# Short-K products as row pairs, and transposes moved to DMA, in a recurrent attention and GLU kernel

## Chip, cores, metric

One core of a Trainium2 chip; the rounds ran on several chips, each with the kernel before beside it. The metric is the device time of the kernel in microseconds (us), as the median of its runs; on one core no slow state appeared in any of the runs below. Engines are named as in the profile: PE is TensorE's products, PEld its weight loads, DVE is VectorE, ACT is ScalarE, POOL is GpSimd, SP issues the DMAs.

## The reference, cut to what matters

Two attention layers with a recurrent memory and two gated layers (GLU) run in the order attention, GLU, attention, GLU over 2048 tokens of width 448. The attention walks through 64 segments of 32 tokens; the memory (8 rows) that a segment's attention puts out is an input of the next segment.

```python
for s in range(n_seg):                       # 64 segments, strictly one after the other
    h = concatenate([mem, x[s]])             # 8 + 32 = 40 rows of 448
    q, k, v = h @ Wq, h @ Wk, h @ Wv         # 16 heads of 256
    p = softmax(mask(q @ k.T * scale))
    o = (p @ v) @ Wo
    mem = o[:8]                              # the recurrence
    outs.append(o[8:])
...
x = x + A(layernorm(x)); x = x + B(layernorm(x))     # twice; B is the GLU
```

## The kernel before

Setup folds the weights: M = Wq Wk^T for each head (448 x 7168 in all), N = Wv Wo. A step then computes T = M h (56 blocks of 128 outputs), scores h T, softmax, U = P h, the new output N U. The two layers run interleaved, layer two 4 segments behind layer one: 68 steps, 60 of which hold both layers (80 columns a product) and 8 only one (40 columns).

The contraction over 448 is cut into four pieces of K: 128, 128, 128 and 64. The fourth piece runs as a product of 128 rows too, of which 64 are zeros:

```python
def t_unit(self, t, c, u0, m):               # m blocks of 128 outputs into one PSUM bank
    ...
        return [MM(b[:, j * n:j * n + n], S.M[:, kt, 16 * c + u0 + j, :],
                   S.hT[:, pp, s, kt, l0:l1, :].rearrange("p l x -> p (l x)"), start=(kt == 0), stop=(kt == 3))
                for j in range(m) for kt in range(4)]
```

LayerNorm results and segment probabilities are transposed on TensorE and copied out of PSUM:

```python
def ln_transpose(self, i, wr):
    T = S.tile("R", 1)
    S.mm(lambda: [MM(T.b().bitcast(BF)[:, c * 128:c * 128 + 128], S.xn[:, i, c * 128:c * 128 + 128], S.ident[:, :], is_transpose=True)
                  for c in range(4)], ...)

def seg_pt(self, t):
    G = S.tile("R", 1)
    S.mm(lambda: [MM(G.b().bitcast(BF)[:, a * 128:a * 128 + 128], S.Ps[:, a, :], S.ident[:, :], is_transpose=True) for a in range(4)], ...)
    S.cp(lambda: S.PTs[:, :], lambda: G.b().bitcast(BF)[:, 0:512], 512, G.res(), [("PTs",)])
```

The hand-off of the recurrence takes the new memory as a sum of two bf16 parts (hi and lo) through small selecting products into hT, which is T's moving operand. Three copies do it, in both kernels:

```python
S.cp(lambda: S.hT[:, pp, s, 0:3, l0:l1, SEG:KEYS], lambda: v()[:, 0:3], 48, ..., eng=("dve",))
S.cp(lambda: S.hT[0:64, pp, s, 3, l0:l1, SEG:KEYS], lambda: v()[64:128, 3], 16, ..., eng=("act",))
S.cp(lambda: S.hT[64:128, pp, s, 3, l0:l1, SEG:KEYS], lambda: v()[64:128, 3], 16, ..., eng=("act",))
```

No instruction order is written down. When the kernel is built, a list scheduler with assumed durations picks, for each engine, the ready operation of the highest priority; a table of constants (`BIAS`) shifts the priority of each kind of work. That computed order, with the semaphores that it needs, is what runs. I call it the plan; it has a length of its own, which is an assumption and not a measurement.

Of the kernel before, what the change touches and what calls it, by code (L numbers as in the profile page):

```python
# [17 lines left out]
SEG = 32  # L18
KEYS = SEG + MEM
NSEG = 64  # L20
F = 1792
# [22 lines left out]
class _Sched:  # L44
# [107 lines left out]
BIAS = {  # L152
    "b_down": -5000.0, "b_layer": 2000.0, "ln_a": 41619.0, "p_t_mem": 500.0, "s_mem": 74990.0, "s_seg": 72560.0,
    "seg_pt": -859.0, "u_mem": -38520.0, "u_seg": 2000.0, "un": -37811.0,
}
# [19 lines left out]
class _Order:  # L175
# [69 lines left out]
    def run(self):  # L245
# [13 lines left out]
        while len(order) < total:  # L259
            best = None  # L260
            for e in self.ENGS:
# [27 lines left out]
                lim = max(f, t0) + (60.0 if e == "pe" else 40.0)  # L289
                t, o = max((x for x in lst if x[0] <= lim), key=lambda x: (x[1].prio, -x[0]))  # L290
                if best is None or (t, -o.prio) < (best[0], -best[2].prio):
# [87 lines left out]
class _Kernel:  # L379
# [16 lines left out]
    def alloc(self):  # L396
        self.M = self.sb("Mw", [128, 4, NO, 128])
        self.N = self.sb("Nw", [128, NO, D])
# [11 lines left out]
        self.TTm = self.sb("TTm", [128, 4, 2, 128])  # L410
        self.hT = self.sb("hT", [128, 2, 2, 4, 2, KEYS])
        self.hK = self.sb("hK", [128, 2, 2, D])
# [3 lines left out]
        self.ys = self.sb("ys", [128, 2, D])  # L416
        self.xBT = self.sb("xBT", [128, 4, 128])
        self.hB = self.sb("hB", [128, NFC, 128])
        self.gT = self.sb("gT", [128, 2, 512])
        self.Es = self.sb("Es", [128, 8, KEYS], F32)  # L420
# [87 lines left out]
    def setup(self):  # L508
# [47 lines left out]
        S.dve(lambda E: E.tensor_scalar(S.ident[:, :], cf[:, 0:128], 0.0, None, op0=ALU.is_equal), 128, [("Es",)], [("ident",)])  # L556
        S.pool(lambda E: E.memset(S.M[64:128, 3, 0:28, :], 0.0), 1800, (), [("Mz", 0)])
        S.dve(lambda E: E.memset(S.M[64:128, 3, 28:56, :], 0.0), 1800, (), [("Mz", 1)])
        for j in range(4):
# [36 lines left out]
        for i in range(H // 2):  # L596
# [13 lines left out]
            for odd in range(2):  # L610
                u, r = i + 8 * odd, slice(64 * odd, 64 * odd + 64)
                S.cp(lambda u=u: S.M[0:64, 3, u:48:16, :], lambda T=T, r=r: T.b()[r, 0:384].rearrange("p (c x) -> p c x", c=3), 384,
                     T.res(half=(odd,)), [("M", 3, u)])
                S.cp(lambda i=i, odd=odd: S.M[0:64, 3, 48 + i, 64 * odd:64 * odd + 64], lambda T=T, r=r: T.b()[r, 384:448], 64,
                     T.res(half=(odd,)), [("M", 3, 48 + i, odd)])
        S.Mkeys = [("M", kt, u) for kt in range(4) for u in range(16)] + [("M", kt, 48 + i, o) for kt in range(4) for i in range(8) for o in range(2)]
        S.Mkeys += [("Mz", 0), ("Mz", 1)]
        S.Nkeys = [("N", o) for o in range(NO)]
# [88 lines left out]
    def qdma(self, name, fn, wr, rd=()):  # L707
        self.q.add("dma", ("sp",), {"sp": 60.0}, fn, rd, wr, name=name)

# [3 lines left out]
    def start_mem(self, l):  # L713

        S = self
        t = LAG * l
        pp, s = (t // 2) % 2, t % 2
        S.cp(lambda: S.hT[:, pp, s, :, l, SEG:KEYS], lambda: S.mTc[:, :, :], 32, [("mTc",)], S.mkeys(pp, s, l, l + 1),
             eng=("pool",))
        r = slice(64 * l + 32, 64 * l + 40)  # L720
        S.cp(lambda: S.hK[r, pp, s, :], lambda: S.mNc[0:MEM, 0:D], D, [("mNc", 0)], [("hKm", pp, s, l)], eng=("pool",))
# [14 lines left out]

    def ln_transpose(self, i, wr):
        S = self
        T = S.tile("R", 1)
        S.mm(lambda: [MM(T.b().bitcast(BF)[:, c * 128:c * 128 + 128], S.xn[:, i, c * 128:c * 128 + 128], S.ident[:, :], is_transpose=True)  # L740
                      for c in range(4)], 4 * S.pitch(128), [("xn", i, 0), ("xn", i, 1), ("ident",)], T.res() + wr)
        return T

    def ln_a(self, p):
        S = self
        pp = p % 2
        S.ln(S.XA[:, p % 4, :], [("XA", p % 4, 0), ("XA", p % 4, 1)], 0, "lnA", 0)
        T = S.ln_transpose(0, [("hTx", pp, s) for s in range(2)])
        for s in range(2):
            S.cp(lambda s=s: S.hT[:, pp, s, :, :, 0:SEG],  # L750
                 lambda s=s: T.b().bitcast(BF)[:, 0:512].rearrange("p (c l s q) -> p c l s q", c=4, l=2, s=2)[:, :, :, s, :],
                 256, T.res(), [("hTx", pp, s)])
        for s in range(2):
            for l in range(2):
                a = 64 * l + 32 * s
                S.cp(lambda a=a, l=l, s=s: S.hK[64 * l:64 * l + 32, pp, s, :], lambda a=a: S.xn[a:a + 32, 0, 0:D], D,
                     [("xn", 0, 0)], [("hKx", pp, s, l)], eng=("pool",))

    def ln_b(self, p):
        S = self  # L760
        S.ln(S.XB[:, p % 2, :], [("XB", p % 2, i) for i in range(3)], 16, "lnB", 1)
        T = S.ln_transpose(1, [("xBT",)])
        S.cp(lambda: S.xBT[:, :, :].rearrange("p a b -> p (a b)"), lambda: T.b().bitcast(BF)[:, 0:512], 512, T.res(), [("xBT",)])


    def t_unit(self, t, c, u0, m):

        S = self
        pp, s = (t // 2) % 2, t % 2
        l0, l1 = S.layers(t)  # L770
        nl = l1 - l0
        n = nl * KEYS
        R = S.tile("R", 1)

        def mms():
            b = R.b()
            return [MM(b[:, j * n:j * n + n], S.M[:, kt, 16 * c + u0 + j, :],
                       S.hT[:, pp, s, kt, l0:l1, :].rearrange("p l x -> p (l x)"), start=(kt == 0), stop=(kt == 3))
                    for j in range(m) for kt in range(4)]

        rd = [("hTx", pp, s)] + S.mkeys(pp, s, l0, l1)
        if t == 0:
            rd = rd + S.Mkeys
        dst = [(nm, c, u0, half) for nm in ("TTm", "TTs") for half in ((0, 1) if c == 3 else (0,))]
        S.mm(mms, 4 * m * S.pitch(n), rd, R.res() + dst)
        src = lambda: R.b()[:, 0:m * n].rearrange("p (o l x) -> p o l x", o=m, l=nl)
        for half in ((0, 1) if c == 3 else (0,)):
# [9 lines left out]

    UNITS = [(3, 0, 4), (3, 4, 4)] + [(c, u, m) for c in range(3) for u, m in ((0, 6), (6, 5), (11, 5))]
    TKEYS = [(c, u, half) for c, u, m in UNITS for half in ((0, 1) if c == 3 else (0,))]

    def s_mem(self, t):
# [4 lines left out]
        C = S.tile("R", 1)  # L806
        S.mm(lambda: [MM(C.b()[:, l * KEYS:l * KEYS + KEYS], S.TTm[:, c, l, :], S.hT[:, pp, s, c, l, :], start=(c == 3), stop=(c == 2))
                      for l in range(l0, l1) for c in (3, 0, 1, 2)], 100.0 * nl,
             [("TTm",) + k for k in S.TKEYS] + [("hTx", pp, s)] + S.mkeys(pp, s, l0, l1), C.res())
        st = S.stat  # L810
# [12 lines left out]
    def s_seg(self, t):  # L823
# [5 lines left out]
        def mms():  # L829
            b = G.b()  # L830
            out = [MM(b[:, 0:8 * KEYS], S.ident[:, :], S.maskr[:, :], start=True, stop=False)]
            for l in range(l0, l1):
                for qd in range(4):
                    for c in (3, 0, 1, 2):
                        out.append(MM(b[:, (qd * 2 + l) * KEYS:(qd * 2 + l) * KEYS + KEYS],
                                      S.TTs[:, c, l, qd * 4:qd * 4 + 4, :].rearrange("p u q -> p (u q)"), S.hT[:, pp, s, c, l, :],
                                      start=False, stop=(l == l1 - 1 and qd == 3 and c == 2)))
            return out
# [22 lines left out]
    def seg_pt(self, t):  # L861
        S = self
        G = S.tile("R", 1)
        S.mm(lambda: [MM(G.b().bitcast(BF)[:, a * 128:a * 128 + 128], S.Ps[:, a, :], S.ident[:, :], is_transpose=True) for a in range(4)],
             4 * S.pitch(128), [("Ps",), ("ident",)], G.res() + [("gseq",), ("PTs",)])
        S.cp(lambda: S.PTs[:, :], lambda: G.b().bitcast(BF)[:, 0:512], 512, G.res(), [("PTs",)])

# [47 lines left out]
    def m_t(self, t):  # L915
# [12 lines left out]
        v = lambda: C.b()[:, 0:64].rearrange("p (c l q) -> p c l q", c=4, l=2)[:, :, l0:l1, :]  # L928
        S.cp(lambda: S.hT[:, pp, s, 0:3, l0:l1, SEG:KEYS], lambda: v()[:, 0:3], 48, C.res(), mk[:-2], eng=("dve",))
        S.cp(lambda: S.hT[0:64, pp, s, 3, l0:l1, SEG:KEYS], lambda: v()[64:128, 3], 16, C.res(half=(1,)), mk[-2:-1], eng=("act",))  # L930
        S.cp(lambda: S.hT[64:128, pp, s, 3, l0:l1, SEG:KEYS], lambda: v()[64:128, 3], 16, C.res(half=(1,)), mk[-1:], eng=("act",))

# [154 lines left out]
    def step(self, t):  # L1087
# [3 lines left out]
        if t > 0:  # L1091
            S.do("m_nat", t)
        for k in S.UNITS:
            S.do("t_unit", t, *k)
        if not last:
# [54 lines left out]
```

## Time and profile before

The median was 1664.21 us in the three runs given at first, and 1664.74 us (1664.17 to 1666.01) in four runs beside the changed kernel.

| | before |
|---|---|
| span of the profiled run | 1662.0 us |
| PE busy | 97% |
| DVE busy | 69% |
| ACT busy | 43% |
| hole of PE in 200 us of the middle | 1.5 us |

The prediction below shows the head, the stretches, the groups and the timeline. What it doesn't show is the list of waits of PE (each line: who waited, for whom, us in total, how often, longest). Most of the long list is setup; of the steps it has

```profile
PE b L127 <- DVE xn L733: 7.0, 31, 1.0
...
PE b L127 <- DVE lo L913: 1.8, 2, 1.5
...
PE b L127 <- DVE Ps L859: 1.7, 2, 1.5
...
PE b L127 <- ACT hT L696: 1.0, 2, 0.7
```

xn and Ps are what the transposes on TensorE wait for. The hand-off of the memory, lo and hT on ACT, is waited for only twice each in the whole run.

### The profile page before, as it was taken

The numbers are of one execution on the slowest core, as the hardware profiler recorded it, in microseconds if no ns is written. First come the engines' busy times: TensorE is split into PE (matmuls) and PEld (weight loads), VectorE is DVE, ScalarE is ACT, GpSimd is POOL, SyncE is SP. The second block draws the span as 40 slices with busy tenths as digits, with TensorE's granted clock in tenths as the row PEclk, the third lists the DMA queues.
The fourth block names the chain that finished last, engine by engine and source line by source line (L and its number), as shares of the span: only waits on it lengthen the run. The fifth ranks groups of instructions, "written<-read, shape, count | busy, mean of one in ns | idle before, by whom it ended". The sixth has DMA issues, their size and how long they took to land. (4 is left out here: it accounts for less than half of the span.)

```text
span 1662.0 us, 68199 instructions
## 1 busy us (share of the span) xinstructions
PE 1614.9 (97%) x30742; PEld 1192.9 (72%) x30742; DVE 1141.2 (69%) x3172; ACT 717.2 (43%) x2051; POOL 93.3 (6%) x156
## 2 busy tenths in 40 slices
PE   5999999999999999999999999999999999999998
PEld 2567777777776777777777777777677777766775
DVE  8757767666767767676776766676676767676665
ACT  4623443445343444544343444434334453433442
POOL 4000000000000000000000000000000000000000
PEclk8999999999999999999999999999999999999999
DMA  9710000000000000000000000000000000000000
GB/s 234 207 40 5 4 3 6 6 5 5 5 5 6 5 4 6 6 4 6 6 5 4 5 5 5 4 6 6 5 6 5 5 6 4 5 3 4 4 4 6
DMA packets 55762, 27.54 MB, mean 17 GB/s; under 512 B 44584, under 2 KB 54576, under 8 KB 55472
## 3 DMA queue, kind: packets, MB, share of 16 engines
q1 hardware_dynamic: 55120, 22.94, 5.7%
q8 instruction: 242, 3.96, 1.0%
q14 instruction: 48, 0.39, 0.1%
q10 hardware_dynamic: 352, 0.24, 0.1%
HBM read 10.33 MB, written 1.84 MB: 7 GB/s over the span
## 5 line engine op out<-in xcount | busy, mean ns | idle before, releaser
L127 PEld LDWEIGHTS b<-hT,Mw 128*128 128x128 bf16 x15232 | 535.2, 100 | 16.9 <-issue 8.6
L127 PE MATMUL b<-hT,Mw 128*128 128x80 bf16 (+1 forms) x15232 | 544.0, 199 | 3.2 <-issue 1.8
L127 PE MATMUL b<-Nw,big 128*64 128x448 bf16 (+1 forms) x1936 | 307.8, 355 | 0.6 <-DVE big L697 0.5
L697 DVE CAST TTs<-b 128x320 bf16<-128x320 f32 (+5 forms) x542 | 244.8, 454 | 13.2 <-PE b L127 12.5
L127 PE MATMUL b<-xBT,big 128*128 128x128 bf16 (+1 forms) x3920 | 217.1, 214 | 0.4 <-DVE lo L913 0.4
L127 PEld LDWEIGHTS b<-xBT,big 128*128 128x128 bf16 x3920 | 203.2, 98 | 7.2 <-ACT UTm L696 4.8
L127 PEld LDWEIGHTS b<-Nw,big 128*64 128x64 bf16 (+1 forms) x1936 | 128.8, 104 | 105.7 <-issue 14.0
L127 PE MATMUL b<-Nw,UTm 128*32 128x448 bf16 x3752 | 193.1, 357 | 2.1 <-DVE UTm L697 1.0
L696 ACT ACTIVATE TTm<-b 64x64 bf16<-64x64 f32 (+5 forms) x338 | 76.7, 227 | 266.7 <-PE b L127 262.7
L1053 DVE TENSOR_TENSOR hB<-gT,b 128x256 bf16<-128x256 bf16 x227 | 91.1, 412 | 119.4 <-ACT gT L1052 108.2
L127 PEld LDWEIGHTS b<-Nw,UTm 128*32 128x32 bf16 x3752 | 100.8, 97 | 88.7 <-issue 15.7
L697 POOL COPY hK<-xn 32x448 bf16<-32x448 bf16 x136 | 75.9, 558 | 1466.9 <-DVE xn L733 1460.4
L696 ACT ACTIVATE TTs<-b 64x256 bf16<-64x256 f32 (+4 forms) x342 | 141.4, 413 | 30.3 <-PE b L127 24.2
L697 DVE CAST TTm<-b 128x80 bf16<-128x80 f32 (+5 forms) x546 | 126.0, 233 | 38.9 <-PE b L127 10.2
L696 ACT ACTIVATE big<-b 128x512 bf16<-128x512 f32 (+1 forms) x242 | 124.5, 555 | 30.7 <-PE b L127 29.9
L697 DVE CAST UTm<-b 128x448 bf16<-128x448 f32 (+2 forms) x124 | 80.2, 647 | 81.0 <-PE b L127 80.1
L1052 ACT ACTIVATE gT<-b 128x256 bf16<-128x256 f32 x227 | 85.6, 380 | 90.7 <-PE b L127 73.0
L697 DVE CAST big<-b 128x512 bf16<-128x512 f32 (+1 forms) x146 | 85.4, 596 | 25.0 <-PE b L127 22.6
L127 PE MATMUL b<-big,hB 128*128 128x448 bf16 (+1 forms) x490 | 98.8, 354 | 0.0
L912 ACT ACTIVATE hi<-b 128x448 bf16<-128x448 f32 x67 | 36.5, 544 | 121.4 <-PE b L127 119.8
L127 PE MATMUL b<-PTs,hK 40*128 40x512 bf16 (+1 forms) x640 | 83.6, 346 | 4.8 <-ACT PTs L696 1.5
L696 ACT ACTIVATE UTm<-b 128x448 bf16<-128x448 f32 (+2 forms) x127 | 64.6, 523 | 24.4 <-PE b L127 23.3
(105 smaller groups left out, 1503.3 us busy)
## 6 DMA issues: line engine op xcount, KB each, us to landing
big<-in_A_Wo_dram SPq DMA_DIRECT2D x3, 896.0 KB, 5.8
out_dram<-ys SPq DMA_DIRECT2D x32, 56.0 KB, 1.9
big<-in_B_W_down_dram SPq DMA_DIRECT2D x1, 1568.0 KB, 7.1
XA<-in_A_x_dram SPq DMA_DIRECT2D x28, 56.0 KB, 2.2
big<-in_B_W_up_dram SPq DMA_DIRECT2D x1, 1344.0 KB, 5.9
big<-in_B_W_gate_dram SPq DMA_DIRECT2D x1, 1344.0 KB, 8.8
Nw<-in_A_Wo_dram SPq DMA_DIRECT2D x1, 896.0 KB, 6.4
XA<-in_A_x_dram ACTq DMA_DIRECT2D x4, 56.0 KB, 4.3
```

The lines of the kernel that those rows point to most:

```text
L127: ins = E.matmul(out, lhsT=lhsT, rhs=rhs, **kw)
L696: return E.activation(out(), src(), ACT.Copy)
L697: return E.tensor_copy(out(), src())
L912: S.act(lambda E: E.activation(S.hi[:, :], C.b()[:, 0:D], ACT.Copy), D, C.res(), [("hi",)])
L1052: S.act(lambda E, k=k, R=R, n=n: E.activation(S.gT[:, k % 2, 0:n], R[0].b()[:, 0:n], ACT.Relu), n, R[0].res(), [("gT", k % 2)])
L1053: S.dve(lambda E, k=k, R=R, n=n, fcs=fcs: E.tensor_tensor(S.hB[:, fcs[0]:fcs[-1] + 1, 0:w], S.gT[:, k % 2, 0:n].rearrange("p (a b) -> p a ...
```

## The change

The intent: pack two 64-row pieces into one pass of the array (rows 0 to 63 and rows 64 to 127 as two tiles), which saves 25 of 224 product slots per step; and take the transposes off TensorE. To keep the number of row-mode switches low, T is cut into a block of six banks, a block of four and one single bank, each paired block starting with its row pairs. The scheduler gets a "stay" bonus for work in the mode that TensorE is in, and a new set of constants.

```diff
 BIAS = {
-    "b_down": -5000.0, "b_layer": 2000.0, "ln_a": 41619.0, ...
+    "b_down": -43294.0, "b_layer": -38803.0, "ln_b": 34745.0, ..., "stay": 42356.0, "t_block": 47423.0, ...
 }
-                t, o = max((x for x in lst if x[0] <= lim), key=lambda x: (x[1].prio, -x[0]))
+                stay = BIAS.get("stay", 0.0) if e == "pe" else 0.0
+                t, o = max((x for x in lst if x[0] <= lim), key=lambda x: (x[1].prio + stay * (x[1].mode == mode), -x[0]))
 ...
-        self.M = self.sb("Mw", [128, 4, NO, 128])
+        self.M = self.sb("Mw", [128, 3, NO, 128])
+        self.M3 = self.sb("M3", [128, 31, 128])
 ...
-        self.hT = self.sb("hT", [128, 2, 2, 4, 2, KEYS])
+        self.hT = self.sb("hT", [128, 2, 4, 2, 2, KEYS])
 ...
-        T = S.ln_transpose(1, [("xBT",)])
-        S.cp(lambda: S.xBT[:, :, :].rearrange("p a b -> p (a b)"), lambda: T.b().bitcast(BF)[:, 0:512], 512, T.res(), [("xBT",)])
+        S.tdma("xBT", lambda: S.xBT[:, :, :], lambda: S.xn[:, 1, :], [("xn", 1, 0), ("xn", 1, 1)], [("xBT",)])
 ...   (the same for xAT, whose DVE copies into hT stay, and for PTs)
+    def tdma(self, name, out, src, rd, wr):
+        self.q.add("dma", ("sp",), {"sp": 1250.0}, lambda E: E.dma_start_transpose(out=out(), in_=src()), rd, wr, name=name, lat=1150.0)
 ...
+    def t_block(self, t, units):
+        ...
+        R = [S.tile("R", 1) for _ in units]
+        pair = len(units) > 1
+        def first():
+            for a, b in zip(range(0, len(units), 2), range(1, len(units), 2)):
+                for j in range(units[a][2]):
+                    for x in (a, b):
+                        c, u0, m = units[x]
+                        side, slot = S.PLACE[16 * c + u0 + j]
+                        h = slice(64 * side, 64 * side + 64)
+                        out.append(MM(R[x].b()[:, j * n:j * n + n], S.M3[h, slot, :], mov(3, h), start=(j == 0), stop=False))
+        if pair:
+            S.mm(first, ..., mode=1)
+        ...   (then the three full-row pieces of each unit, and its copies)
 ...
-    UNITS = [(3, 0, 4), (3, 4, 4)] + [(c, u, m) for c in range(3) for u, m in ((0, 6), (6, 5), (11, 5))]
+    BLOCKS = [[(3, 0, 4), (3, 4, 4), (0, 0, 6), (1, 0, 6), (0, 6, 5), (0, 11, 5)], [(1, 6, 5), (1, 11, 5), (2, 6, 5), (2, 11, 5)], [(2, 0, 6)]]
```

Two things that this cut leaves out. The scheduler's assumed time for issuing a plain load or store on SP goes from 60 to 500 ns, so the two plans differ in an assumption as well. And the dependency keys of hT are now kept per layer (`("hTx", pp, s, l)`), but the segment scores still name their read of hT by the old key `("hTx", pp, s)`, which nothing writes any more: neither the plan nor a semaphore holds the next copies into hT back until these products have read it. In the changed kernel's trace those copies come at least 45 us after the products, so nothing went wrong; with another order it could.

## The prediction

> **What bounds the kernel now.** I read the page's head first, then the busy table by stretches, then the groups kept apart by form, then the timeline of one step.
>
> ```profile
> span 1662.0 us, 68199 instructions
> PE 1614.9 (97%) x30742; PEld 1192.9 (72%) x30742; DVE 1141.2 (69%) x3172; ACT 717.2 (43%) x2051; POOL 93.3 (6%) x156
> ```
>
> TensorE is busy for 97% of the span, VectorE for 69%, ScalarE for 43%. Busy time counts each product's latency, so I looked for real holes: in the stretches table (columns: stretch, its length, then busy time and count by engine) the middle of the run has about 1.5 us of hole in 200.
>
> ```profile
> 0.00:120.00 120.00, 97.02 (x1299) 53.53 (x1300) 84.99 (x245) 51.85 (x144) 21.67 (x27) 0.93 0.68 166
> ...
> 700.00:900.00 200.00, 198.46 (x3791) 149.57 (x3784) 137.63 (x376) 85.25 (x242) 10.56 (x19) 1.00 0.02 5
> ...
> 1500.00:1662.00 162.00, 151.07 (x3024) 110.17 (x3020) 98.37 (x295) 61.09 (x185) 6.70 (x12) 0.99 0.02 5
> ```
>
> Only the setup (23 us of hole) and the last 162 us (11 us) are not full. So the time is the time in which TensorE issues products, and a removed product is worth its pitch, not its duration. The groups concerned (by form: engine, operation, operands, shapes, count, busy us, mean ns, then idle us before them and what ended it):
>
> ```profile
> L127 PE MATMUL b<-hT,Mw 128*128 128x80 bf16 x13440 | 496.0, 202 | 0.7 <-ACT hT L696 0.7
> ...
> L127 PE MATMUL b<-ident,xn 128*128 128x128 bf16 x276 | 27.7, 224 | 11.1 <-DVE xn L733 7.0 <-DVE seln L569 4.1
> L127 PE MATMUL b<-ident,Ps 128*128 128x128 bf16 x272 | 26.7, 220 | 1.7 <-DVE Ps L859 1.7
> ...
> L127 PE MATMUL b<-hT,Mw 128*128 128x40 bf16 x1792 | 48.0, 180 | 2.5 <-issue 1.8 <-ACT hT L696 0.3 <-DVE hT L697 0.2
> ```
>
> 13440 is 60 steps with both layers times 56 blocks of T times 4 pieces of K; 1792 is the 8 one-layer steps. 276 is four transposes for each of 69 LayerNorms, 272 four for each of 68 steps. The timeline gives the pitches.
>
> ```profile
> 799.90 8.19 PE L127 MATMUL b<-hT,Mw 128*128 128x80 bf16 x224
> ```
> ```profile
> 831.18 5.52 PE L127 MATMUL b<-xBT,big 128*128 128x128 bf16 x96
> ```
>
> The mean duration of a T product is 202 ns, so 224 of them start within 8.19 - 0.20 = 7.99 us: 7.99/223 = 36 ns each. For the 128-column product it is (5.52 - 0.22)/95 = 56 ns, which I use for a transpose of the same shape. From the starts of all T products in the trace the one-layer ones (40 columns) come every 27 ns.
>
> **What the Trainium skill says.** "TensorE: Matmul & The Clock Gate", section "Back-to-back issue gap", gives N/2.4 + 2.5 ns: 35.8 ns for 80 columns, 55.8 for 128. The trace agrees (36 and 56). Its table has about 25 ns for anything up to 64 columns; the trace's 27 agrees.
>
> "TensorEngine Tiling (Array Packing)", "Key Properties", says that tiles run in parallel and that changing the tiling mode drains the engine. Both are in this trace. The memory path already runs row pairs (40 rows, 128 columns, two layers) and here are the first six:
>
> ```profile
> 813.27 0.34 PE L127 MATMUL b<-PTm,hK 40*128 40x128 bf16 x6
> ```
>
> Six products, 0.34 - 0.22 = 0.12 us from first start to last; at 56 ns in series it would be 0.28. In the records the two of a pair start 3 ns apart and pairs 55 ns apart, so a pair costs one pitch. And the price of a switch:
>
> ```profile
> 820.36 0.35 PE L127 MATMUL b<-Nw,big 128*128 128x448 bf16 x1
> 820.64 0.30 PE L127 MATMUL b<-PTs,hK 40*64 40x256 bf16 x4
> 820.88 0.24 PE L127 MATMUL b<-hT,Mw 128*128 128x80 bf16 x2
> ```
>
> 448 columns stream in 0.19 us, but the next start is 0.28 later: 0.09 lost. The four 256-column products run together in 0.11, the next start is 0.24 later: 0.13 lost. I counted over the trace from 120 us on: 716 places where the rows or columns in use change, together 94 us above the streaming time, at best about 95 ns each (68 us) and 26 us of real waiting. That is 10.5 switches per step.
>
> "VectorE: DVE Perf Modes", "The three transpose paths", gives 1309 ns for a 128x128 DMA transpose against 390 on TensorE. No run here has one from on-chip memory yet; what the trace has is 896 KB transposes out of device memory in setup, below.
>
> **The change part by part.**
>
> *Row pairs.* T's fourth K piece holds 64 live rows and 64 zero rows. The change packs two such pieces into one array pass, each in its half. Block one has 30 of the 56 output blocks, block two 20, both paired; the last 6 stay as they were. 25 pairs replace 50 products, so 25 slots fall away: 25 x 36 ns = 0.90 us per two-layer step, x 60 = 54 us. One-layer steps: 25 x 27 ns = 0.67 us, x 8 = 5 us. Sum 59 us, if a pair of 80 columns costs 36 ns.
>
> *Transposes.* 548 x 56 ns = 31 us of TensorE slots go. With them go the waits of TensorE right before them, 7.0 (LayerNorm) and 1.7 (segment) from the group lines: 9 us. Beside that, 67 ScalarE copies of 595 ns into PTs and 33 of 597 ns into xBT go (60 us), which TensorE doesn't wait for.
>
> *Switches.* Two blocks per step that go into row mode and out again would be 4 x 68 = 272 more, x 95 ns = 26 us. Against it: the transposes are full-array work that often sits between two packed groups (in the trace 32 follow the 32-column products of the recurrence, 31 precede the segment pairs), perhaps 80 switches (8 us); and the new bias that keeps the order in the mode it is in should put T's pairs next to the segment and memory pairs, which have the same form, and segment pairs next to each other. I take the remaining 18 us as about half won back: +9 us.
>
> *New waits.* DMA: 896 KB took 5.9 us to land in setup, a 56 KB store 1.9, so a 128 KB one is, as an estimate, 1.9 + 4.0/7 = 2.5 us. From Ps to the first segment product the trace has a median of 4.2 us, of which 1.5 us are between the copy and the product; xn to the GLU's first product 2.2 us. Two steps of slack lie behind each of these in the middle of the run, so nothing there; in the tail, where one chain is left, two or three of them lie bare: +3 us. Block one claims six of the eight PSUM banks at once, and must wait until six are free: +5 us, my least certain term. Setup: 32 copies more into the packed weights, beside a loading stage: +2 us.
>
> Sum: -59 - 31 - 9 + 9 + 3 + 5 + 2 = -80, from 1664 to 1584 us.
>
> **The rivals.**
>
> 1. *A pair costs two issue slots.* "TensorEngine Tiling (Array Packing)", "Instruction Overhead", puts a floor of some 60 cycles on each product (25 ns). If that floor is one of issue, not of each tile, a pair costs 50 ns: 22 saved per pair, 60 x 25 x 22 = 33 us, nothing in one-layer steps. The six-product line speaks against it for a burst that stood queued; no long run of short pairs is in this trace. It would give about 1610.
>
> 2. *Six banks at once starve.* T's block can't start until six banks are free together; the GLU and segment work take two at a time. T heads the recurrence (T, scores, softmax, U, next memory), whose non-TensorE part is some 5 us per step from the timeline, hidden under filler now. If 0.5 us per step becomes bare it is 34 us: about 1615. The page shows nothing on it.
>
> 3. *Evictions become the bound in T.* VectorE takes 0.24 + 0.48 = 0.72 us for a unit of five (TTm and TTs), as long as TensorE took for its 20 products; now a unit comes every 0.6 us. ScalarE at 43% and 60 us lighter can take the difference, so I give it 5 us at most.
>
> 4. *Switches are not won back, or fall much more.* +26 without any gain: 1601. If the bias leaves a third fewer than the 716, that is 239 x 95 ns = 23 us less than before in place of 9 more: 1552.
>
> **Range and chances.** The certain part is 31 us of transposes plus at least 33 of pairs less 26 of switches: 38 us, 2.3%. Rivals 1 and 2 together with no switches won back would leave it within 2%. Nothing that I see makes it slower than before, as DVE and ACT lose work. I take 1584 us, 1552 to 1622 for 8 in 10; faster by over 2% 0.91, within 0.07, slower 0.02.
>
> **What will show it.** T's products: 10080 + 6 x 60 = 10440 full two-layer ones and 3000 of 64 rows, with paired starts 3 to 4 ns apart and pairs 36 ns apart (rival 1: 50). No product on ident with xn or Ps; 137 DMA transposes of 2 to 3 us. Switches per step about 10. TensorE's holes per 200 us still near 1.5; if they are 5 or more, with VectorE or ScalarE evictions named as what ended them, rival 2 or 3 holds. It is wrong above all if the order of the work, which is rearranged as a whole, brings more waiting than the pairs save.

## The result, and the profile after

The changed kernel took 1626.69 us in the median (1624.73 to 1631.09, 4 runs), the kernel before 1664.74 us in the same rounds. The ratio is 0.9774, with a 95% interval of 0.9752 to 0.9796. Ratios here are the mean time of one kernel's fast runs over that of the other's of the same rounds, so they are not quite the ratios of the medians; where I compare two kernels from different rounds, I take the difference of their ratios times 1663 us. Both intervals enter such a difference, so it is uncertain by some 5 us. The result is right. The time fell by 38 us, not by 80, and lies above the range.

The head of the page of the changed kernel:

```profile
span 1622.9 us, 67486 instructions
...
PE 1548.5 (95%) x30194; PEld 1116.4 (69%) x30194; DVE 1071.2 (66%) x2987; ACT 717.3 (44%) x2164; POOL 90.6 (6%) x156
```

548 products are gone, as many as there were transposes, and PE's busy time fell by 66 us, more than the span did. Its share fell from 97% to 95%, so there is idle time that was not there before. The stretches (length, then busy time and count of PE, PEld, DVE, ACT, POOL, then clock, DMA share and GB/s) show where:

```profile
0.00:120.00 120.00, 94.30 (x1269) 51.42 (x1270) 79.08 (x256) 51.40 (x157) 19.23 (x27) 0.91 0.72 172
...
700.00:900.00 200.00, 195.82 (x3797) 142.13 (x3796) 132.10 (x355) 89.52 (x266) 8.89 (x16) 1.00 0.08 16
...
1500.00:1623.00 123.00, 108.19 (x2242) 79.25 (x2234) 67.14 (x210) 40.77 (x138) 4.45 (x8) 0.96 0.10 18
```

The hole in the middle grew from 1.5 us to 4.2 us in 200, and the last stretch has 15 us of hole in 123 where the kernel before had 11 in 162. DVE and ACT stand at 132 and 90 us of 200: neither is full.

The groups of T, by form:

```profile
L128 PE MATMUL b<-hT,Mw 128*128 128x80 bf16 x10080 | 400.7, 202 | 9.4 <-DVE big L703 7.8 <-DVE hT L703 1.6
...
L128 PE MATMUL b<-hT,M 64*128 64x80 bf16 x3000 | 74.6, 199 | 3.7 <-DVE TTs L703 3.7
...
L128 PE MATMUL b<-hT,M 128*128 128x80 bf16 x360 | 55.1, 202 | 0.0
```

The counts are the predicted ones: 10080 + 360 full products and 3000 of 64 rows. The idle time in front of T, 0.7 us before, is now 9.4 + 3.7. One block of pairs in the timeline (start, length, count):

```profile
806.48 0.71 PE L128 MATMUL b<-hT,M 64*128 64x80 bf16 x30 [0.27 <-DVE TTs L703]
807.13 0.35 PE L128 MATMUL b<-hT,Mw 128*128 128x80 bf16 x5
```

30 products of 0.20 us start within 0.71 - 0.20 = 0.51 us, so the 15 pairs come every 0.51 / 14 = 36 ns: a pair costs one slot. (In the records the two of a pair start 3 to 4 ns apart.) The DMA issues (count, then us from issue to landing):

```profile
PTs<-Ps SPq DMA_TRANSPOSE x68, 2.4
xBT<-xn SPq DMA_TRANSPOSE x35, 2.7
xAT<-xn SPq DMA_TRANSPOSE x34, 2.4
```

137 of them, within 0.2 us of the estimate of 2.5. And the list of waits of PE:

```profile
PE b L128 <- DVE big L703: 19.0, 31, 0.7
PE b L128 <- DMA xBT<-xn: 9.0, 6, 5.9
...
PE b L128 <- DVE lo L947: 5.9, 16, 1.5
...
PE b L128 <- DVE TTs L703: 3.7, 14, 0.3
```

The waits for xn and Ps are gone and others are there. "big" is U, the copies of the segment products out of PSUM: PE waits for them before more segment products and, by the profile, before T. lo is the hand-off, waited for 16 times instead of 2. One such place in the timeline of PE, and DVE and ACT at the same time:

```profile
846.91 0.35 PE L128 MATMUL b<-lo,seln 128*128 128x448 bf16 x1
847.78 0.27 PE L128 MATMUL b<-hT,Mw 128*128 128x80 bf16 x3 [0.52 <-DVE big L703]
```
```profile
847.08 0.68 DVE L703 CAST big<-b 128x512 bf16<-128x512 f32 x1
```
```profile
846.30 0.62 ACT L702 ACTIVATE big<-b 128x512 bf16<-128x512 f32 x1
846.78 0.42 ACT L702 ACTIVATE UTm<-b 128x256 bf16<-128x256 f32 x1
847.26 0.38 ACT L702 ACTIVATE hT<-b 64x16 bf16<-64x16 f32 x2
```

T starts at 847.78 (its first weight load at 847.75), 0.11 us after the second of the two short hT copies on ACT ends (847.26 + 0.38 = 847.64). The copy of U that the profile names runs on DVE until 847.08 + 0.68 = 847.76, so it can't have released the load: the releaser is inferred, and here it is the wrong one. The hT copies stand behind two copies of segment products on ACT.

### An account over all products

I went over the starts of all TensorE products from the fifth to the 64th masking product of the segment scores (59 two-layer steps) and split each gap between successive starts. Streaming is N/2.4 + 2.6 ns for N columns, at least 25 ns: the formula of the kernel's own scheduler, which the pitches of 36 and 56 ns bear out. Products that run side by side share one such time. Where the rows or columns in use change, 95 ns are put down to the switch (close to the smallest losses measured). The rest is waiting. How side-by-side products are counted moves the levels of streaming and waiting by up to 10 us, but their differences by only 2.

| us | before | after | difference | predicted for the same |
|---|---|---|---|---|
| streaming | 1309.9 | 1230.0 | -79.9 | -79 (52.8 pairs, 26.4 transposes) |
| switches | 60.7 (639) | 76.5 (805) | +15.8 | +9 |
| waiting | 31.5 | 48.8 | +17.3 | -4 (-9 and +5) |
| 59 steps | 1402.1 | 1355.2 | -46.9 | -74 |
| before them | 149.8 | 149.2 | -0.6 | |
| after them | 106.4 | 114.8 | +8.4 | |
| both ends | | | +7.8 | -6 (-6 pairs, -4 or -5 transposes, +3 tail, +2 setup) |

The sum of the differences, -39.1 us, is that of the spans (1662.0 and 1622.9); the last row of times ends with the last product, and 3.7 us of copies and stores follow in both kernels. By the work that each wait stands before, and the operation that ended last of those it needed, the 59 steps after have 12.4 us for copies of segment products ahead of further segment products, 10.3 for the hT copies ahead of T, 9.4 for lo ahead of the selecting products, and 4.7 for T's own copies ahead of its six-bank block (14 times 0.34 us; the block of 30 products above, which comes last of the three in time). In the kernel before, the copies of segment products (2.2), hT (1.4) and lo (2.7) were small.

The theory at this point: the slots were won as predicted, and half of them were lost to waits and switches of the rearranged order. The rivals: a pair is dearer than it looks, DMA landing times are bare, six banks at once starve T, or evictions are the bound.

### The profile page after: what moved, and what is told of

It reads as the page before. It is cut to its first block, busy times and chain, and to the rows that moved or that the text cites. A ratio compares the mean times of both kernels' runs of the same rounds, so it can differ in the third digit from the quotient of the medians.

```text
span 1622.9 us, 67486 instructions
## 1 busy us (share of the span) xinstructions
PE 1548.5 (95%) x30194; PEld 1116.4 (69%) x30194; DVE 1071.2 (66%) x2987; ACT 717.3 (44%) x2164; POOL 90.6 (6%) x156
## 5 line engine op out<-in xcount | busy, mean ns | idle before, releaser
L128 PE MATMUL b<-hT,Mw 128*128 128x80 bf16 (+1 forms) x11424 | 440.6, 200 | 10.4 <-DVE big L703 7.8
L128 PEld LDWEIGHTS b<-hT,Mw 128*128 128x128 bf16 x11424 | 418.6, 100 | 33.2 <-DVE big L703 13.1
L703 DVE CAST TTs<-b 128x320 bf16<-128x320 f32 (+5 forms) x423 | 192.2, 454 | 31.9 <-PE b L128 30.9
L702 ACT ACTIVATE TTs<-b 64x256 bf16<-64x256 f32 (+4 forms) x461 | 191.7, 416 | 39.7 <-PE b L128 31.5
L702 ACT ACTIVATE TTm<-b 128x80 bf16<-128x80 f32 (+5 forms) x400 | 91.7, 229 | 224.6 <-PE b L128 223.8
L128 PE MATMUL b<-hT,M 64*128 64x80 bf16 (+3 forms) x3808 | 139.9, 197 | 6.8 <-DVE TTs L703 3.7
L703 DVE CAST big<-b 128x512 bf16<-128x512 f32 (+1 forms) x163 | 107.3, 675 | 58.3 <-PE b L128 57.2
L703 DVE CAST UTm<-b 128x448 bf16<-128x448 f32 (+2 forms) x107 | 64.8, 615 | 101.2 <-PE b L128 99.9
L128 PEld LDWEIGHTS b<-hT,M 64*128 64x128 bf16 (+1 forms) x3808 | 105.8, 97 | 22.3 <-DVE hT L703 6.7
L702 ACT ACTIVATE big<-b 128x512 bf16<-128x512 f32 (+1 forms) x225 | 106.4, 514 | 8.4 <-PE b L128 7.5
```

Source lines behind the costliest of these rows:

```text
L128: ins = E.matmul(out, lhsT=lhsT, rhs=rhs, **kw)
L702: return E.activation(out(), src(), ACT.Copy)
L703: return E.tensor_copy(out(), src())
```

## The experiments

Eighteen runs in six sets; all results compared as correct. Kernels that are wrong on purpose (half-wide copies) are named; the comparison let them pass as well, so it can't be taken as a test of them, and it is a weak test of the others.

### 1. Pairs undone in the same order: same_order_unpaired

The order is the changed kernel's, product by product; each half of a pair runs as a full-row product against a weight piece with zeros.

```diff
-        self.M3 = self.sb("M3", [128, 31, 128])
+        self.M3 = self.sb("M3", [128, 56, 128])
 ...
-                        h = slice(64 * side, 64 * side + 64)
-                        out.append(MM(R[x].b()[:, j * n:j * n + n], S.M3[h, slot, :], mov(3, h), start=(j == 0), stop=False))
+                        out.append(MM(R[x].b()[:, j * n:j * n + n], S.M3[:, slot, :], mov(3, slice(0, 128)), start=(j == 0), stop=False))
```

> The changed kernel in its own order of work, DMA transposes kept, but the 50 paired products of each step run as full-row products against zero rows (25 slots more per step, no mode switch inside T; a wrong result is not expected). If the time is TensorE's slots plus switches: +54 us in the two-layer steps and +5 in the others for the slots, minus about 240 switches inside T x 95 ns = 23 us, so +34 to +36: about 1662 us, level with the kernel before. Rival, the time freed by pairing only turns into waits on evictions and on the recurrence: +17 us or less, at most 1644 us.

1657.61 us, ratio 0.9973 (0.9957 to 0.9990): 33 us slower than the changed kernel. In the account, streaming is 50.7 us more (1280.7) and 221 switches are fewer (584), 21 us at 95 ns. Pairs gain what the slots say, less two switches for each of the two blocks. The waiting is 48.2 us, as in the changed kernel (48.8), although TensorE has 50 us more to stream. That fits waiting that belongs to the order, but doesn't show it alone: the slots went back into T, and the work beside the hand-offs, where most of the waits lie, stayed the same.

### 2. Each DMA transpose doubled: twice_xAT, twice_xBT, twice_PTs

A dummy transpose into a spare buffer goes ahead of each, so that the real one is issued one issue time (1.19 us in the trace) later.

```diff
+                if o.name in ('xAT',):
+                    ...
+                    self.sc.dma("twice", lambda E, k=k: E.dma_start_transpose(out=k.spare[:, :, :], in_=k.xn[:, 0, :]), res(o.rd), [("spare",)], eng=o.fixed)
                 self.sc.dma(o.name, o.fn, res(o.rd), res(o.wr), eng=o.fixed)
```

> The changed kernel in its own order, with a second, unused DMA transpose issued ahead of each of the 34 that feed hT, so that these land about 1.2 us later (its issue takes 1.19 us on the queue). If the loop through the second layer (GLU, residual, LayerNorm, T of a later step) is where TensorE waits in the steady part, nearly half to all of the 34 delays show: +17 to +40 us, 1643 to 1666. Rival, the landing is hidden and the waits come from evictions: within 5 us of the changed kernel's 1627.

> The same doubling for the 35 transposes that feed the GLU. The GLU is filler work in the middle, but its result is the second layer's input: if that loop has no slack left, +10 to +40 us; if the GLU's start has slack, only the tail shows it, +2 to +5 us.

> The same doubling for the 68 transposes of the segment probabilities. The segment products come microseconds after the landing in the trace, so only the tail should show: +1 to +5 us, 1628 to 1632. Rival, they hold the order up in each step: +40 to +80 us.

They took 1671.45, 1669.97 and 1657.79 us, ratios 1.0055, 1.0044 and 0.9975 (intervals of at most 0.0024 to each side), which is 47, 45 and 33 us more than the changed kernel: each above what was expected, and for PTs, where only the tail was to show it, a clear miss. The waits of PE of the three kernels, in this order:

```profile
PE b L128 <- DVE hT L708: 39.0, 33, 2.5
```
```profile
PE b L128 <- DMA xBT<-xn: 48.7, 34, 7.2
```
```profile
PE b L128 <- DMA PTs<-Ps: 23.0, 21, 2.3
```

39.0 us over 33 waits is 1.2 us each: nearly all of the lengthening shows. The landing is hidden in the changed kernel (apart from the tail, TensorE waits some 5 us for all three together) but it is hidden without slack; the plan places the reader just where the assumed landing ends (1.25 + 1.15 = 2.4 us after the issue). "Two steps of slack lie behind each of these in the middle of the run" is wrong for this order.

### 3. One part alone: pairs_only, dma_only; and blocks2, same_order_hT_pool

pairs_only puts the transposes back on TensorE; dma_only runs T unpaired in single banks. Both with ordering constants searched anew by the length of the plan.

```diff
 # pairs_only
-        S.tdma("pts", ...)      (and xAT, xBT)
+        S.mm(lambda: [MM(G.b().bitcast(BF)[:, a * 128:a * 128 + 128], S.Ps[:, a, :], S.ident[:, :], is_transpose=True) for a in range(4)], ...)
+        S.cp(lambda: S.PTs[:, :], lambda: G.b().bitcast(BF)[:, 0:512], 512, G.res(), [("PTs",)])
 # dma_only
-    BLOCKS = [[(3, 0, 4), (3, 4, 4), (0, 0, 6), (1, 0, 6), (0, 6, 5), (0, 11, 5)], ...]
+    BLOCKS = [[(3, 0, 4)], [(3, 4, 4)], [(0, 0, 6)], [(0, 6, 5)], ...]
```

> Row pairs without the DMA transposes: LayerNorm and segment transposes back on TensorE, order of work found anew by the same search over the kernel's own bias table. The order has about 220 more mode switches than before. Slots: -59 us; switches +220 x 95 ns = +21. If waits stay as they were: -38 us, about 1625 (level with the whole change). If pairing brings waits of its own (six banks claimed at once): 1640 or above.

> DMA transposes without pairing (T unpaired, one bank per unit), order found anew by the same search; about 100 switches fewer than before. Slots: -31 us, switches -9: if waits stay as they were, 1624. If the landing of 2.4 us in place of some 1.1 us on TensorE is what brings the new waits: 1640 or above. Together with pairs_only: if the two parts are independent, their gains should add to the whole change's 38 us; if both alone give 35 or more, the shortfall comes only from having both.

1658.30 us (0.9976, 0.9961 to 0.9991) and 1656.22 us (0.9969, 0.9946 to 0.9992): each part alone is worth 4 to 5 us, both together 38. Streaming fell by 52.2 us in pairs_only and by 30.1 in dma_only, but the waiting is 60.0 and 58.3 us, twice that of the kernel before. So a part's slots come out near the prediction, and most of them are eaten in each of the two. The whole change, with 48.8 us, waits less than either part alone; by the account that is why 5 and 4 make 38.

blocks2 cuts T's paired blocks into five of two banks, so that no block claims more than two.

```diff
-    BLOCKS = [[(3, 0, 4), (3, 4, 4), (0, 0, 6), (1, 0, 6), (0, 6, 5), (0, 11, 5)], [(1, 6, 5), (1, 11, 5), (2, 6, 5), (2, 11, 5)], [(2, 0, 6)]]
+    BLOCKS = [[(3, 0, 4), (3, 4, 4)], [(0, 0, 6), (1, 0, 6)], [(0, 6, 5), (0, 11, 5)], [(1, 6, 5), (1, 11, 5)], [(2, 6, 5), (2, 11, 5)], [(2, 0, 6)]]
```

> The changed kernel with T's pairs in five blocks of two banks instead of one of six and one of four (the order's search prefers to put blocks that follow each other in one mode together, so the number of switches stays within 1% of the change's). If the claim of six banks at once is what makes TensorE wait: 10 us or more below the changed kernel's ratio of 0.977. If not: within 0.5% of it.

1639.91 us, 0.9853 (0.9834 to 0.9873), 13 us slower than the changed kernel. Its waiting is 56.5 us, with the same three hand-offs on top (12.9, 10.5 and 9.4 us). The 4.7 us ahead of the six-bank block are gone, but TensorE now waits 9 us ahead of 512-column segment products, where it waited under 2. The claim of six banks at once has its price, and it is not where most of the waits come from.

same_order_hT_pool moves the two DVE copies from xAT into hT to GpSimd, in the same order.

```diff
-                self.sc.op(o.fixed, (lambda E, o=o: o.fn(E, o.fixed)), res(o.rd), res(o.wr))
+                e = "pool" if ("xAT",) in o.rd else o.fixed
+                self.sc.op(e, (lambda E, o=o, e=e: o.fn(E, e)), res(o.rd), res(o.wr))
```

> The changed kernel in its own order, but the two copies from the landed LayerNorm transpose into hT are done by GpSimd instead of VectorE, so that VectorE's queue doesn't stand behind the landing (it idled 11.2 us there in the profile). If that blocks VectorE's evictions and so T: up to 11 us faster, ratio near 0.971. If GpSimd's slower copy, or its place behind the hK copies, delays T's start more: slower by 5 us or more.

1632.92 us, 0.9826 (0.9809 to 0.9844): 9 us slower, the second of the two outcomes named: freeing DVE of them brought no gain, and the copies take 398 ns each on GpSimd against 223 on DVE.

### 4. The order searched with measured durations: replanned

The same work, with the ordering constants and three of the plan's assumptions fitted to the durations of the trace.

```diff
-BIAS = {"b_down": -43294.0, "b_layer": -38803.0, "ln_b": 34745.0, ...}
+BIAS = {'b_down': -9955.2, 'b_layer': -10001.6, 'ln_b': -63110.2, ..., 'hop': 53.9, 'ovl': 74.4, 'tlat': 957.1}
```

> The changed kernel, nothing changed but the order: the bias table (and three constants of the ordering: overlap of neighbouring copies, landing time, hop to TensorE) searched again, with orders judged by the durations and gaps that the traces so far show. If the shortfall lies in the order (waits and switches that a better order avoids): 10 us or more below the changed kernel, ratio 0.970 or less (1613 us or less). If the waits are inherent in the chain of work per step: within 0.3% of the changed kernel's 0.977.

1635.97 us, 0.9833 (0.9818 to 0.9848), 10 us slower: a miss. One transpose in each group of four steps is issued close behind the store of an output. In SP's queue and on PE:

```profile
868.91 0.50 SPq L1109 DMA_DIRECT2D out_dram<-ys  x1
870.64 1.19 SPq L760 DMA_TRANSPOSE xAT<-xn  x1
```
```profile
874.97 0.28 PE L128 MATMUL b<-hT,Mw 128*128 128x80 bf16 x3 [1.36 <-DVE hT L699]
```

That transpose landed 4.0 us after its issue, not 2.4, and T waited 1.36 us. That the store is the cause is not shown: in the same trace transposes of Ps landed after about 4 us too with nothing issued in the 7 us before them (4.2 us for the one issued at 721.97). And this plan assumes a landing after 1.25 + 0.96 = 2.2 us, while none in its trace took less than 2.39. A plan without slack pays for every landing above its assumption.

### 5. Evictions and another order: half-wide copies, repaired

T's copies into TTs half as wide, in each kernel (wrong on purpose):

```diff
-            S.cp(lambda h=h, v0=v0: S.TTs[h, c, l0:l1, v0:v0 + m, :].rearrange("p l u q -> p u l q"),
-                 lambda h=h: src()[h, :, :, 0:SEG], ...)
+            z = [("TTsz",)]
+            S.cp(lambda h=h, v0=v0: S.TTs[h, c, l0:l1, v0:v0 + m, 0:SEG // 2].rearrange("p l u q -> p u l q"),
+                 lambda h=h: src()[h, :, :, 0:SEG // 2], ...)
```

> The changed kernel in its own order, wrong on purpose: the copies of T into TTs write half their columns (some 0.15 to 0.3 us less each, 884 of them), TensorE's work unchanged. If VectorE's and ScalarE's evictions now hold TensorE up (its waits rose from 31 to 49 us in the two-layer steps): 15 us or more faster, 1610 or less, ratio 0.968 or less. If the waits come from elsewhere (switches, recurrence, landing): within 5 us of the changed kernel's 1625.

> The same halving in the kernel before, in its own order, wrong on purpose. In it VectorE alone keeps up with T (0.72 us per unit of five against TensorE's 0.72), so the gain should be under 8 us, ratio 0.995 or more. If it gains as much as the changed kernel does, evictions are no new bound and the shortfall isn't theirs.

1620.16 us (0.9742, 0.9724 to 0.9760), 5 us below the changed kernel; and 1665.62 us (1.0009, 1.0002 to 1.0015) in the kernel before. T's evictions hold back some 5 us, hardly clear of the noise and the amount that the prediction set as the upper end of rival 3; they are not the bound.

The copies of the segment products half as wide, in each kernel (wrong on purpose):

```diff
-                S.cp(lambda l=l, key=key, c=c, nh=nh: key[l][0][:, c * 16:c * 16 + nh, :],
+                S.cp(lambda l=l, key=key, c=c, nh=nh: key[l][0][:, c * 16:c * 16 + nh, 0:SEG // 2],
```

> The changed kernel in its own order, but the evictions of the segment products (the copies into U and UTm) copy half of their columns; the result is wrong on purpose. Theory A (evictions in a burst ahead of the memory hand-off and on the banks): the waits of TensorE for them (12 us), for the lo copy (9 us) and for the hT copies (10 us) fall by more than half, the time falls by 15 to 30 us, to about 1600 us, ratio to the kernel before near 0.961. Rival B (the hand-off's own chain): the time falls by under 6 us, ratio 0.974 or more.

> The same half-wide segment evictions in the kernel before, wrong on purpose. Both theories: its waits for these evictions are small (2 us) and its segment products come spread out, so the time stays within 5 us of before, ratio 0.997 to 1.001. If it falls by as much as the changed kernel, the evictions are no part of the difference.

1623.39 us (0.9755, 0.9740 to 0.9769) and 1651.37 us (0.9925, 0.9909 to 0.9942). The first is only 3 us below the changed kernel, within the noise, the second 12 us below the kernel before: the reverse of theory A. The waits for lo went (9.4 to 2.9 us), those for the banks fell (12.4 to 8.1), but T still waited 9.5 us for hT, and DVE's LayerNorm work became another wait of T (1.9 to 4.6). Queues of segment copies in front of the hand-off are real, as the ACT timeline above shows, but taking them away moves the wait on.

repaired is the changed kernel with 14 changes of its order in the steady steps: ten kinds of operations put just before or behind another one, four given to the other copying engine. They were found with a replay of the order that uses durations of the trace.

```diff
+MOVES = [['m_nat', 3, 0, 'un', 19, -1], ['ln_a', 8, 3, 't_block', 22, 3], ['eng', 't_block', 28, 1, 'act'], ...]
         self.q.run()
+        self.q.moved(MOVES)
         self.q.emit()
```

> The changed kernel, with the same work and the same blocks; 14 kinds of operations of the steady steps stand at another place in the order or on the other of the two copying engines (found with a replay of the order that uses the durations of the trace). If the added waiting is a matter of this order: about 10 us below the changed kernel, 1608 to 1620 us, ratio to the kernel before 0.967 to 0.974, with fewer waits for the lo and hT copies. If the waiting is inherent in the change or sits in jitter that the replay does not have: within 3 us of the changed kernel, or slower, as the replanned one was.

1619.34 us, 0.9734 (0.9714 to 0.9754): 7 us below the changed kernel, inside the range expected. In the account it has 28 switches fewer (777), and about 44 us of waiting instead of 48.8. It computes the right result and is the fastest correct version of this study. Part of the loss is a matter of the order, then, but a small part of it was found.

### 6. Where the slack is, and whether plans are to be believed: doubled hand-off, other orders

The two short ACT copies of the hand-off, done twice:

```diff
-                self.sc.op(o.fixed, (lambda E, o=o: o.fn(E, o.fixed)), res(o.rd), res(o.wr))
+                for _ in range(2 if o.cat == "m_t" and o.fixed == "act" else 1):
+                    self.sc.op(o.fixed, (lambda E, o=o: o.fn(E, o.fixed)), res(o.rd), res(o.wr))
```

> The changed kernel in its own order, with each of the two short copies of the new memory on ScalarE done twice in a row: the hand-off from the memory products to T becomes longer by about two copies, 0.38 us by the profile, per step, and nothing else is added for TensorE. Theory: the hand-off has no slack left in most steps; at least 0.2 us per step show, 12 to 23 us in all, about 1640 to 1650 us, ratio to the kernel before near 0.988. Rival: it is bare in one step of four only, where the trace has its waits (15 of them): 15 times 0.38 = 6 us, about 1632 us, ratio near 0.981.

> The same doubled copies in the kernel before. Theory: there the hand-off has slack (TensorE waits for it 1.4 us in all), so at most 5 us are added, ratio 0.999 to 1.003. If it costs as much as in the changed kernel (12 us or more, ratio 1.007 and above), the hand-off was as tight before, and its lost slack is no part of the shortfall.

1645.73 us (0.9889, 0.9872 to 0.9905), 19 us more than the changed kernel, and 1683.72 us (1.0121, 1.0104 to 1.0138), 20 us more than the kernel before. The longest of the new waits in the steps, of the kernel before and of the changed one:

```profile
PE b L127 <- ACT hT L697: 13.7, 34, 1.1
```
```profile
PE b L128 <- ACT hT L703: 16.5, 19, 0.9
```

My theory falls: the hand-off was just as tight before, although it showed only 1 us of waiting there. A small wait in the profile doesn't prove slack.

Last, each kernel with other ordering constants, chosen only by the length of the plan and by being different (36% and 44% of neighbouring TensorE operations differ):

```diff
 # before_other_order
-    "b_down": -5000.0, "b_layer": 2000.0, "ln_a": 41619.0, "p_t_mem": 500.0, "s_mem": 74990.0, ...
+    'b_down': -5000.0, 'b_layer': -2646.0, 'ln_a': 0.0, 'p_t_mem': 500.0, 's_mem': 33424.2, ..., 't_unit': 30709.7
 # after_other_order
-    "b_down": -43294.0, "b_layer": -38803.0, "ln_b": 34745.0, ..., "stay": 42356.0, "t_block": 47423.0, ...
+    'b_down': -19300.0, 'b_layer': -44657.8, 'ln_b': 0.0, ..., 'stay': 36930.5, 't_block': 52839.6, ...
```

> The kernel before with other ordering constants, the same work; 36% of TensorE's neighbouring pairs differ, and the plan's own length is 1647 us against 1646. Theory: the small distance of chip and plan in the kernel before (18 us) belongs to that one order, and another order of the same planned length shows the 35 to 45 us that every replanned kernel so far has shown: 1682 to 1692 us, ratio 1.011 to 1.017. Rival: the change itself makes plans less true (landing times, pair mode); then this one stays near 1647 + 18 = 1665 us, ratio 0.997 to 1.003.

> The changed kernel with other ordering constants, the same work; 44% of TensorE's neighbouring pairs differ, the plan's own length is 1596 us against 1586. Both theories: 35 to 45 us above its plan, 1631 to 1641 us, ratio 0.980 to 0.986. If it comes out within 25 us of its plan (under 1621 us), the changed kernel's own order was an unlucky one.

1667.28 us (1.0022, 1.0012 to 1.0033) and 1646.22 us (0.9897, 0.9880 to 0.9913). The rival holds for the kernel before, and the changed kernel came out 5 us above the range that both theories gave: another order of the kernel before stays 20 us above its plan, as its own does (18), and the other order of the changed kernel is 50 us above its plan (own order: 41). The waits of the changed kernel in the other order:

```profile
PE b L128 <- DVE lo L943: 17.3, 41, 1.5
PE b L128 <- DVE UTm L699: 16.5, 17, 1.0
```

The first is the same hand-off, longer. The second, the copies of U's memory part, is another one: the products that wait for it waited 0.2 us in the changed kernel's own order. Beside the plans, over the 59 steps:

| | planned idle of TensorE | measured waiting | switches planned, measured |
|---|---|---|---|
| before | 20.1 | 31.5 | 566, 639 |
| before_other_order | 21.3 | 31.2 | 569, 642 |
| after | 24.2 | 48.8 | 719, 805 |
| after_other_order | 33.8 | 67.1 | 688, 774 |
| pairs_only | 23.6 | 60.0 | 769, 827 |
| dma_only | 26.4 | 58.3 | 493, 538 |

The kernel before waits 10 to 11 us more than planned, in two orders; all four orders with any part of the change wait 25 to 36 us more. This is systematic, not a lucky order.

## Why the prediction was wrong, point by point

**Right: the slots.** "25 slots fall away: 25 x 36 ns" and "548 x 56 ns" came out at 79.9 us of streaming against 79. That agreement is in part luck: the parts alone gave 52.2 and 30.1 against 52.8 and 26.4. Pairs come every 36 ns, so rival 1 (two issue slots per pair) is dead, by the timeline and by same_order_unpaired. The waits for xn and Ps went. The landing of a transpose was 2.4 to 2.7 us against an estimate of 2.5; luck helped there too, as 5.9 us is the quickest of four groups of 896 KB transposes (up to 8.7 us, which would have given 2.9). Two small readings of the prediction are off and carry nothing: its 27 ns for one-layer products is a mean with a few waits in it (the median is 25), and from xn to the GLU's first product the trace has 2.0 us about as often as 3.0, not 2.2.

**Mis-sized: switches.** "+9 us" was 15.8 us: 166 more in the 59 steps, 13.0 per step over the run against 10.5. 221 switches lie inside T, close to the four per step expected, and only 55 were won back elsewhere, where I had taken some 180 in the whole run (17 of 26 us).

**Failed: "New waits".** This is the step that sank the range. It named two sources of waits in the middle of the run, landings and the claim of six banks, and took the rest as it stood in the order of the kernel before: -9 and +5 us. Those came out: the waits for xn and Ps went, and the six-bank block waits 4.7 us. Landings, put at nothing, hold TensorE up for some 5 us of the 59 steps. What had no term are the hand-offs in an order that is planned anew: waiting for copies of segment products rose from 2.2 to 12.4 us, for hT from 1.4 to 10.3, for lo from 2.7 to 9.4. That is 26 us; other, smaller waits fell by some 9, and the sum was +17 instead of -4. I took the small waits of the kernel before as a property of the work. They were a property of an order that fits its chip to 10 us: the doubled hand-off shows that it had no slack even before. The two steps of slack behind each transpose, which the doubled transposes refute, are the 5 us. The prediction's own last sentence, that it is wrong if the order "brings more waiting than the pairs save", is what happened by half.

**Failed: the tail.** "+3 us" stood for bare landings; the stretch after the 59 steps grew by 8.4 us, where slots should have shortened it. Its waits went from 3.1 to 12.3 us, 8.7 of them for xBT before the GLU. But of the three such waits (5.9, 1.6 and 0.9 us) at most 4.9 us are landing, not far from the +3. The longest wait, 5.9 us, ends with the last of these lines (SP's queue, then PE):

```profile
1609.63 1.19 SPq L764 DMA_TRANSPOSE xBT<-xn  x1
```
```profile
1594.93 3.44 PE L128 MATMUL b<-xBT,big 128*128 128x64 bf16 x112 [1.64 <-DMA xBT<-xn]
1612.06 5.75 PE L128 MATMUL b<-xBT,big 128*128 128x64 bf16 x112 [5.86 <-DMA xBT<-xn]
```

The landing is the 2.4 us from 1609.63 on. The other 3.4 us are residual sums and LayerNorm on DVE and ACT with nothing left for TensorE, work that in the kernel before ran beneath other products. And the same 112 products took 5.75 us instead of 3.44: the granted clock was 0.55 of full speed there, 1.00 before. So 2.3 us of the tail are clock, in the one execution that was profiled.

**Rivals.** Rival 2 had the size (0.3 us more waiting per step) but not the cause: the six-bank block itself waits 4.7 us, and blocks2, with two banks at a time, waits no less in all. Rival 3 is worth 5 us (after_half_evict). Rival 4 was half true.

**The sum.** Against the prediction: 7 us of switches, 21 of waits in the middle and 14 at the two ends, less 1 of streaming, make 41: what lies between -80 and the -39 of the spans. That the gain equals the 38 us that the prediction called its certain part is chance: that part counts 33 us for the pairs, which brought over 50, and no new waits.

**What stays open.** Why every order with a part of the change waits 25 us and more above its plan is not settled. It is not the six-bank claim, not T's evictions, not segment evictions alone, not lost slack in the hand-off, and not the luck of one order. Nor are the copies slower: on DVE, those into U take 681 and 685 ns before and after, those into TTs 481 and 483, lo 615 in both. That TensorE has less to stream beside the hand-offs is not excluded. What all four orders share, and the kernel before lacks, is the "stay" bonus, under which ready work of another mode is put off, the longer assumed issue of loads and stores, and the new layouts of hT and of the fourth piece of the weights. No run separates these; that one of them is the cause would only be argued.

## What to carry to other kernels

A slot that falls away on a full engine is worth its pitch, and in this case that was predicted well. But when the order is planned anew, the waits of the old order are no guide: ask of each hand-off how much a lengthening would cost, by lengthening it, since a hand-off without a wait may have no slack at all. Price both parts of a change alone and together; here 4 and 5 us alone, each with an order of its own, made 38 together.

## What the Trainium skill lacked or had wrong

- "VectorE: DVE Perf Modes", section "The three transpose paths", gives 1309 ns for a 128x128 DMA transpose. What a reader needs for hiding one is the time from issue to landing: 2.4 us in the median for 128x512 from on-chip memory (2.7 for xBT), 1.19 us of it in the issuing queue, and over 3.8 us for 28 of the 129 that replanned issues from 150 us on. That section doesn't give it, and no page gives this spread for transposes.
- "TensorEngine Tiling (Array Packing)", section "Key Properties", says that a change of mode drains the engine, without a price. Here a switch cost about 95 ns at best, and the changed kernel has 805 of them in 59 steps, 76 us.
- "TensorE: Matmul & The Clock Gate", section "Back-to-back issue gap", puts the sustained spacing of load and product at about 81 ns for 128 columns and calls its formula that of an isolated gap. In this case 96 such products, each with its own weight load, came every 56 ns, which is the formula.
